# The second layer of an expert: two of its three blocks by seven half-width products

## The chip, the cores and the metric

The kernel runs on one core of a Trainium2 chip. The metric is the device time of one execution in microseconds (us). Engines are named as the profile names them: PE is TensorE, DVE VectorE, ACT ScalarE, POOL GpSimd, SP SyncE (which issues the DMAs).

## What is computed

A gated linear attention makes the rows x, a mixture of experts follows. All is fp32 at the interface.

```python
# q, k, v, f_logit: (4, 8, 768, 48)
f = sigmoid(f_logit)
for t in range(768):
    state = f[:, :, t, :, None] * state + einsum('bhd,bhe->bhde', k[:, :, t], v[:, :, t])
    y[:, :, t] = einsum('bhd,bhde->bhe', q[:, :, t], state)
x = y.transpose(0, 2, 1, 3).reshape(3072, 384)

P = exp(x @ w_gate - max)               # 3072 x 8, then 8 rounds of row and column normalisation
for e in range(8):
    h = maximum(x @ w1[e], 0)           # w1[e]: 384 x 1024
    out += P[:, e:e + 1] * (h @ w2[e])  # w2[e]: 1024 x 384
```

## The kernel before

**Products.** Each fp32 product is made of three fp16 ones: both factors are split into a high and a low part (names that end in h and l), and high by high, low by high and high by low are accumulated in PSUM. `mm` issues every matmul; all of them carry its line, L285 (L287 after).

**Stages.** Up to about 491 us the attention, the gate and experts 0 and 1 are computed. Then comes the main loop over `ORDER`: 48 periods, one for each of experts 2 to 7, half m of their 1024 hidden units, and batch b of 768 rows. A period n does layer one of its (e, m, b), and the layer two of period n−1.

**Layer one** treats the 768 rows as three blocks t of 256 tokens and the weights as a grid of blocks too, and gets all from 15 products (`SLOTS`), each 128 columns of weights (twice, c = 0 and 1) by 256 tokens: 15 x 2 x 3 = 90 matmuls of 256 columns. They go into six PSUM banks A to F, tiles kb_n_A to kb_n_F. `EVENTS` says after which slot which step on the banks follows; slots 15 to 21 are slots 0 to 6 of the next period (`pending`). The steps, in `event`: copy of a bank to a tile cp (ACT, L1354), add of such a copy to a bank (DVE, L1356), init of a bank from another and a copy (DVE, L1359), move of bank B into C (ACT, L1362), sum (DVE, L1365). A bank ends as one hidden block, half f of the columns and token block t: then hh makes kh, the high fp16 part after the maximum with 0 (ACT, L1384), and hl makes kl, the low part (DVE, L1387).

**Layer two** (`layer2`) has two ways for a block of 256 tokens. `plain(t, v)` makes 128 rows by 12 matmuls of 384 columns into a PSUM tile kyps. `paired(t)` makes both its 128-row halves at once by seven products instead of eight, each 192 columns wide, in 42 matmuls, into two PSUM tiles kxps and kyps (px and py), each with two halves (x0, x1, y0, y1). Its left factors are kah and kal (one half of the block: ga, ACT L1376; gb, DVE L1378) and four sums and differences kf of the hidden halves (hs makes kr on ACT, L1370; gs makes the four kf on DVE, L1374), split into kgh (gh, ACT L1380) and kgl (gl, POOL L1382; DVE in the last period). Its right factors are w2 and four sums of its blocks, k2s, split into k2sh and k2sl. While the products run, ACT copies three of them into part (L1240), POOL adds parts and makes one half of both (L1249, L1250), DVE makes the other half (L1252); when the products are done, DVE adds both to x1 (L1255) and to py (L1259). Block 1 is paired; blocks 0 and 2 are plain.

**Eviction.** Results go to acc, scaled by the gate: either by one DVE instruction (direct, L1211), or by ACT into yt (L1214) and POOL's add (L1215). Two of the six halves of a period are direct.

**Order.** `pin` chains instructions on DVE, ACT and POOL in the order of the code, `mm` does so on PE. `layer2` is a generator which `drain` advances after each slot by a fixed number of units, so that layer-two matmuls stand between layer-one products; it is started at slot `LAG` = 2. `postpone` puts a step off by so many slots. The table `plan` (through `at_slots`) gives to slots what else is done: weight preparation for later periods (`prepare_w1`; `prepare_w2`; `prepare_pairs`, which loads w2 a second time as k2rs and makes the sums k2s), conversion of the last batch's rows (`converts[3]`, xah3 and xal3), adding back the first two experts' results from DRAM (`readds`), and checks of the inputs' ranges (`guard`, `first_maxima`, `verdict`) that set a flag.

Of the kernel before, what the change touches and what calls it, by code (L numbers as in the profile page):

```python
# [73 lines left out]
END = 22  # L74
ORDER = [(e, m, b) for e in range(2, NE) for m in range(2) for b in range(B)]
PLAIN, PAIRED = (0, 2), 1
# [180 lines left out]
def fast(ctx, tc, qkf, vbd, wg, w1, w2, out, flag):  # L257
# [565 lines left out]
    def verdict():  # L823
# [14 lines left out]
        for n, (col, op) in enumerate(((5, ALU.min), (4, ALU.max), (2, ALU.max), (6, ALU.min), (0, ALU.min))):  # L838
            rows.append(partition_reduce(nc, cst, psm, "m", identf, g[:, col:col + 1], op, f"gd{n}", mm, pin))
            yield  # L840
            yield
# [170 lines left out]
    def prepare_w1(e, j):  # L1012
# [10 lines left out]
        for part in (WSUMS[:5], WSUMS[5:]):  # L1023
# [19 lines left out]
    def prepare_w2(e, j, maxima_last=False):  # L1043
# [6 lines left out]
        if not maxima_last:  # L1050
            maxima_()
        wh, wl = (lp.tile([128, 2, DM], F16, name=f"k2{n}_{e}_{j}", tag=f"k2{n}", bufs=4) for n in "hl")
        pin(nc.scalar.activation(out=wh, in_=raw, func=AF.Copy, scale=W2S))
        yield
        for g in range(2):
            pin(nc.vector.scalar_tensor_tensor(out=wl[:, g], in0=raw[:, g], scalar=W2S, in1=wh[:, g], op0=ALU.mult, op1=ALU.subtract))
            if g:
                k2[e, j] = wh, wl
            yield
        if maxima_last:  # L1060
            maxima_()
            yield

    def prepare_pairs(e, j):
        raw = raw_weights(e, 2, j, "s")
        yield
        sums = raw_tile(f"k2s_{e}_{j}").rearrange("p (r d) -> p r d", d=DH)
        (b11, b12), (b21, b22) = ((raw[:, f, 0:DH], raw[:, f, DH:DM]) for f in range(2))
        for n, x, op, y in ((0, b12, ALU.subtract, b22), (1, b12, ALU.subtract, b11)):
            pin(nc.gpsimd.tensor_tensor(out=sums[:, n, :], in0=x, in1=y, op=op))  # L1070
        yield
        for n, x, op, y in ((2, b11, ALU.subtract, sums[:, 0, :]), (3, b21, ALU.subtract, sums[:, 2, :])):
            pin(nc.gpsimd.tensor_tensor(out=sums[:, n, :], in0=x, in1=y, op=op))
        yield
        wh, wl = (lp.tile([128, 4, DH], F16, name=f"k2s{n}_{e}_{j}", tag=f"k2s{n}", bufs=2) for n in "hl")
        pin(nc.scalar.activation(out=wh, in_=sums, func=AF.Copy, scale=W2S))
        yield
        pin(nc.vector.scalar_tensor_tensor(out=wl, in0=sums, scalar=W2S, in1=wh, op0=ALU.mult, op1=ALU.subtract))
        k2s[e, j] = wh, wl
        yield  # L1080
# [32 lines left out]
    while True:  # L1113
# [18 lines left out]
        if step == 46:  # L1132
            work.append(chained(prepare_w1(ORDER[0][0], j) for j in range(2)))
# [35 lines left out]
    def layer2(n, h):  # L1169
# [17 lines left out]
        def plain(t, v):  # L1187
            ps = room(f"kyps_{n}_{t}_{v}")
            i = 0
            for f in range(2):  # L1190
                for c in range(2):
                    wh, wl = k2[e, 2 * m + c]
                    hh, hl = h[f, t]
                    for a, w in ((hh, wh), (hl, wh), (hh, wl)):
                        mm(out=ps, lhsT=a[:, c, 128 * v:128 * v + 128], rhs=w[:, f, :], start=(i == 0), stop=(i == 11))
                        i += 1
                        if i < 12:
                            yield 1
# [19 lines left out]
        def product(out, left, right, start=False, stop=False):  # L1218
            for c in range(2):
                if left is None:  # L1220
                    a = [x[:, c, :] for x in h['a']]
                elif left[0] is None:
                    a = [x[:, left[1], c, :] for x in h['g']]
                else:
                    a = [x[:, c, 128 * left[1]:128 * left[1] + 128] for x in h[1, PAIRED]]
# [8 lines left out]
        def paired(t=PAIRED):  # L1234
            px, py = (room(f"k{q}ps_{n}").rearrange("p (s d) -> p s d", s=2) for q in "xy")
            x0, x1, y0, y1 = (ps[:, i, :] for ps in (px, py) for i in range(2))
            part, both = (lp.tile([128, k, DH], F32, name=f"{x}_{n}", tag=x, bufs=1) for x, k in (("part", 3), ("both", 2)))
# [4 lines left out]
            yield from product(x0, None, (0, 0), start=True)  # L1242
            yield from product(x1, (None, 1), (None, 1))
            copy(0, x0)
            yield from product(y0, (None, 0), (None, 0), start=True)
            copy(1, x1)
            yield from product(y1, (None, 2), (None, 2))
# [3 lines left out]
            yield from product(x0, (1, 0), (1, 0))  # L1251
            pin(nc.vector.tensor_tensor(out=both[:, 0, :], in0=y1, in1=part[:, 0, :], op=ALU.add))  # L1252
            yield from product(x1, (None, 3), (1, 1), stop=True)
            yield from product(y0, (1, 1), (None, 3), stop=True)
# [3 lines left out]
            late = n < len(ORDER) - 1  # L1258
            postpone(late, lambda: pin(nc.vector.tensor_tensor(out=py, in0=py, in1=both, op=ALU.add)))  # L1259
# [4 lines left out]
        ends = len(halves) - (n == len(ORDER) - 1)  # L1264
        for half in halves[:ends]:
            yield from plain(*half)
        yield from paired()
        for half in halves[ends:]:
            yield from plain(*half)
# [35 lines left out]

    for n, (e, m, b) in enumerate(ORDER):
        q, c = n // 4, n % 2
        if q + 1 < PERIODS // 4 and not c:
            e2, m2, _ = ORDER[n + 4]
            gen = prepare_w1(e2, 2 * m2 + n % 4 // 2)  # L1310
            at_slots(n, (0, 5, 5, 6, 9, 11, 13) if n else (0, 5, 5), gen)
            at_slots(n + 1, (2, 5, 7, 11, 12, 13, 14) if not n else (11, 13, 14) if not n % 4 else (4, 6, 8), gen)
        if n == 0:
            at_slots(0, (1, 2, 4, 5, 12), prepare_w2(e, 2 * m, True))
            late_w2 = prepare_w2(e, 2 * m + 1, True)
            at_slots(0, (4, 6, 8, 11), late_w2)
# [181 lines left out]
```

## Time and profile before

| | |
|---|---|
| median of 3 runs | 1522.49 us (1522.18 to 1523.27) |
| the profiled execution | 1523.2 us |
| its span in the trace, mean granted clock | 1521.5 us, 0.996 |
| main loop's first matmul of bank F, period 2 | 546.27 us |
| the same, period 43 | 1413.34 us |
| last matmul of the main part | 1512.04 us |

Starts in the trace count from the span's start. A row of a timeline has start, duration, engine, line, operation, tile written, tiles read, shape, count, and in brackets the idle time before it with what ended it. A row of a group has count, busy time, mean duration in ns, idle time before and what ended it. Tile names have their numbers left out there, so kf stands for kf of all periods.

### The profile page before, as it was taken

Reading aid. Unit: us, or ns where it says so; the run is one execution under the profiler, and the core shown is the slowest. Engines: PE = TensorE matmul, PEld = TensorE weight load, DVE = VectorE, ACT = ScalarE, POOL = GpSimd, SP = SyncE. Lnnn points to the kernel's source line nnn. Section 1 sums busy time; section 2 is a strip of 40 time slices with the busy share of each in tenths; the row PEclk is TensorE's granted clock in tenths of the full one; section 3 lists DMA queues with packets and bytes.
Section 4 is the critical chain, followed back from the end, with each engine's and each line's share of the span. In section 5 each row is a group of like instructions: output and inputs, shape, how many; then the busy total and the mean of one; then the engine's idle time right before and its main releaser. Section 6 shows DMA issues by size and latency. Waiting matters only on the chain.

```text
span 1521.5 us, 35282 instructions
## 1 busy us (share of the span) xinstructions
PE 1495.7 (98%) x14321; PEld 1159.2 (76%) x14321; DVE 1146.4 (75%) x2014; ACT 903.8 (59%) x1815; POOL 764.0 (50%) x964
## 2 busy tenths in 40 slices
PE   7999999999999999999999999999999999999997
PEld 5788877666666787788877888788887888878885
DVE  8878888985775877877777777768677776767664
ACT  6655555653343766666666666666566656566553
POOL 1244444546429245566665656455454545454433
PEclk9999999999999999999999999999999999999999
DMA  9455554541001122222222121101020101010012
GB/s 277 113 136 134 136 129 112 141 115 34 27 22 63 53 75 64 66 58 83 64 79 69 58 74 33 53 21 54 22 63 12 42 22 42 23 32 22 11 59 71
DMA packets 86239, 105.15 MB, mean 69 GB/s; under 512 B 50256, under 2 KB 66768, under 8 KB 86064
## 3 DMA queue, kind: packets, MB, share of 16 engines
q1 hardware_dynamic: 86064, 102.78, 24.2%
q8 instruction: 114, 1.87, 0.5%
q14 instruction: 61, 0.50, 0.1%
HBM read 78.97 MB, written 14.16 MB: 61 GB/s over the span
## 4 chain that ended last, share of the span: by engine, by line
PE 91%; DVE 5%; ACT 1%; issue 1%; POOL 0%; DMA 0%; POOLq 0%; DVEq 0%; ACTq 0%
PE kyps L285 29%; PE yps L285 13%; PE hps L285 10%; PE kb_A L285 8%; PE kb_B L285 8%; PE kxps L285 6%; PE kb_D L285 6%; PE kb_C L285 4%; PE kb_E L285 2%; PE kb_F L285 2%; PE kvps L285 1%; PE aps L285 1%; DVE w2l L357 0%; DVE hl L438 0%; DVE w1l L357 0%
## 5 line engine op out<-in xcount | busy, mean ns | idle before, releaser
L1215 POOL TENSOR_TENSOR acc<-acc,yt 128x384 f32<-128x384 f32 x175 | 176.7, 1010 | 303.2 <-ACT yt L1214 186.3
L285 PEld LDWEIGHTS <-k1h 128*128 128x128 f16 x2880 | 281.7, 98 | 52.7
L285 PE MATMUL kyps<-k2h,kh 128*128 128x384 f16 x768 | 250.4, 326 | 0.1
L285 PE MATMUL kyps<-k2h,kl 128*128 128x384 f16 x768 | 250.4, 326 | 0.0
L285 PE MATMUL kyps<-k2l,kh 128*128 128x384 f16 x768 | 250.4, 326 | 0.0
L285 PEld LDWEIGHTS <-kh 128*128 128x128 f16 x1920 | 186.4, 98 | 67.2
L1214 ACT ACTIVATE yt<-kyps,pes 128x384 f32<-128x384 f32 x175 | 101.6, 581 | 122.5 <-PE kyps L285 81.0
L285 PEld LDWEIGHTS <-k1l 128*128 128x128 f16 x1440 | 140.8, 98 | 43.4 <-issue 7.9
L285 PE MATMUL yps<-w2h,hl 128*128 128x384 f16 x384 | 125.4, 327 | 2.8 <-DVE hl L438 2.6
L285 PE MATMUL yps<-w2l,hh 128*128 128x384 f16 x384 | 125.5, 327 | 1.9 <-DVE w2l L357 1.9
L285 PE MATMUL yps<-w2h,hh 128*128 128x384 f16 x384 | 125.5, 327 | 0.2 <-ACT hh L435 0.2
L285 PEld LDWEIGHTS <-w1h 128*128 128x128 f16 x1344 | 97.1, 98 | 34.1 <-issue 3.1
L1382 POOL TENSOR_TENSOR kgl<-kf,kgh 128x512 f16<-128x512 f32 x94 | 111.8, 1189 | 19.0 <-DVE kl L1387 11.1
L285 PEld LDWEIGHTS <-kl 128*128 128x128 f16 x960 | 93.9, 98 | 32.3 <-issue 0.3
L285 PEld LDWEIGHTS <-hh 128*128 128x128 f16 x768 | 74.6, 98 | 47.7 <-issue 2.5
L1354 ACT ACTIVATE cp<-kb_A 128x512 f32<-128x512 f32 x144 | 86.1, 598 | 25.9 <-DVE kb_A L1356 24.6
L285 PE MATMUL hps<-xl,w1h 128*128 128x128 f16 (+1 forms) x672 | 84.1, 257 | 1.2 <-DVE xl L647 0.6
L285 PE MATMUL hps<-xh,w1l 128*128 128x128 f16 (+1 forms) x672 | 84.9, 258 | 0.0
L285 PE MATMUL hps<-xh,w1h 128*128 128x128 f16 (+1 forms) x672 | 83.6, 257 | 0.4 <-DVE hl L389 0.3
L285 PE MATMUL kb_A<-xbh,k1h 128*128 128x256 f16 x288 | 78.5, 272 | 0.5 <-ACT cp L1354 0.4
L285 PE MATMUL kb_A<-xbl,k1h 128*128 128x256 f16 x288 | 78.5, 273 | 0.0
L285 PE MATMUL kb_A<-xbh,k1l 128*128 128x256 f16 x288 | 78.5, 273 | 0.0
(291 smaller groups left out, 4516.9 us busy)
## 6 DMA issues: line engine op xcount, KB each, us to landing
q<-in_qkf_dram SPq DMA_DIRECT2D x23, 672.0 KB, 5.2
vr<-in_vbd_dram SPq DMA_DIRECT2D x24, 384.0 KB, 3.5
k1r<-in_w_dram SPq DMA_DIRECT2D x24, 384.0 KB, 3.1
ys<-yr SPq DMA_DIRECT2D x48, 192.0 KB, 2.8
k2r<-in_w_dram SPq DMA_DIRECT2D x24, 384.0 KB, 3.1
yb<-ys SPq DMA_DIRECT2D x48, 192.0 KB, 2.4
k2rs<-in_w_dram SPq DMA_DIRECT2D x24, 384.0 KB, 3.0
out_dram<-acc SPq DMA_DIRECT2D x24, 192.0 KB, 1.9
```

Of the source, the lines that this page charges most:

```text
L285: ins = (nc.tensor.transpose if transpose else nc.tensor.matmul)(**kw)
L1214: pin(nc.scalar.activation(out=yt, in_=ps, func=AF.Copy, scale=p))
L1215: pin(nc.gpsimd.tensor_tensor(out=y, in0=y, in1=yt, op=ALU.add))
L1354: pin(nc.scalar.activation(out=fresh(ev[2]), in_=bk, func=AF.Copy))
L1382: pin((nc.vector if tag == str(PERIODS - 1) else nc.gpsimd).tensor_tensor(out=hs['g'][1][:, ev[1]:ev[2]], in0=hs['f'][:, ev[1]:ev[2]], in1 ...
```

## The change

Blocks 0 and 1 are paired, block 2 alone is plain. Per period 24 matmuls of 384 columns go and 42 of 192 come. The order inside a layer two is now paired(0), two plain halves, paired(1); in the first period the plain halves come first, in the last the second plain half comes last. Block 0's step hs to gl are done from banks A and B, those of block 1 as before from E and C, and block 0's first half has no kh and kl any more. The py add follows the eviction of px in the same step, and the eviction of py the step after; they were one and two steps late.

The raw w2 is loaded once: `prepare_w2` makes k2 and k2s from one load, `prepare_pairs` goes. The slots of the weight preparation, the conversion of the last batch, the readds (two per period from period 3 on), the maxima and the checks are new. The five matmuls of `verdict` are issued between layer-two matmuls of the last three periods. At the end of the loop the remaining steps follow the order `ENDING`.

```diff
+EVENTS = {..., 8: (('move', 'C', 'B'), ('hs', 'A', 0)),
+          9: (('ga', 'A', 0),), 10: (('copy', 'C', 7), ('gs', 'A', 0, 0), ('gb', 'A', 0)), 11: (('add', 'D', '-', 7),),
+          12: (('init', 'F', '+', 1, 'D'), ('hh', 'B', 1, 0)), 13: (('gs', 'B', 0, 1), ('gs', 'B', 0, 2), ('gs', 'B', 0, 3)),
+          14: (('gh', 0, 0, 2), ('gl', 0, 0, 2), ('sum', 'D', '-', 4, 3), ('hl', 'B', 1, 0)), 15: (('add', 'C', '+', 3), ('hh', 'D', 1, 2), ('gh', 0, 2, 4), ('gl', 0, 2, 4)),
+          16: (('hh', 'C', 1, 1), ('hh', 'F', 0, 2), ('hl', 'D', 1, 2), ('ga', 'E', 1)), 17: (('hs', 'E', 1), ('hl', 'F', 0, 2)),
+          18: (('gs', 'E', 1, 0), ('gb', 'E', 1)), 19: (('gs', 'C', 1, 1), ('gs', 'C', 1, 2), ('gs', 'C', 1, 3)),
+          20: (('gh', 1, 0, 2), ('gl', 1, 0, 2), ('hl', 'C', 1, 1)), 21: (('gh', 1, 2, 4), ('gl', 1, 2, 4))}
+ENDING = (('add', 'gh', 'gl'), ('ga', 'hs', 'hh'), ('gs',), ('gb', 'hl'), ('gh', 'gl', 'late'))
-PLAIN, PAIRED = (0, 2), 1
+PLAIN, PAIRED = (2,), (0, 1)
...
-            late = n < len(ORDER) - 1
-            postpone(late, lambda: pin(nc.vector.tensor_tensor(out=py, in0=py, in1=both, op=ALU.add)))
-            postpone(2 * late, lambda: evict(t, 1, py, False))
+            pin(nc.vector.tensor_tensor(out=py, in0=py, in1=both, op=ALU.add))
+            postpone(n < len(ORDER) - 1, lambda: evict(t, 1, py, False))
             yield PAUSE
-        halves = [(t, v) for t in PLAIN for v in range(2)]
...
+        parts = [lambda: paired(0), lambda: plain(2, 0), lambda: plain(2, 1), lambda: paired(1)]
+        if n == len(ORDER) - 1:
+            parts[2:] = parts[:1:-1]
+        if not n:
+            parts = parts[1:3] + parts[::3]
+        for part in parts:
+            yield from part()
...
-            drain((24 * len(PLAIN) + 42 * PAIR_COST + PAUSE) / PRODUCTS)
+            drain((24 * len(PLAIN) + (42 * PAIR_COST + PAUSE) * len(PAIRED)) / PRODUCTS)
```

What this does to the order, at three places. First DVE where period 8 passes into period 9, and period 7's layer two ends. Before, from the half of both to kl of bank F:

```order
L1252 TENSOR_TENSOR both_7_10919<-kyps_7_10917,part_7_10918 128x192
L1356 TENSOR_TENSOR kb_8_C_10842<-kb_8_C_10842,cp8_3_10980 128x512
L1255 TENSOR_TENSOR kxps_7_10916<-kxps_7_10916,both_7_10919 128x192
L1211 SCALAR_TENSOR_TENSOR acc3_9480<-kxps_7_10916,pes_114,acc3_9480 128x384
L1374 SCALAR_TENSOR_TENSOR kf_8_10861<-kb_8_C_10842,kr_8_10864 128x256
L1374 SCALAR_TENSOR_TENSOR kf_8_10861<-kb_8_C_10842,kf_8_10861 128x256 x2
L1259 TENSOR_TENSOR kyps_7_10917<-kyps_7_10917,both_7_10919 128x384
L1387 SCALAR_TENSOR_TENSOR kl_8_1_2_10678<-kb_8_D_10749,kh_8_1_2_10677 128x512
L1387 SCALAR_TENSOR_TENSOR kl_8_1_1_10676<-kb_8_C_10842,kh_8_1_1_10675 128x512
L1356 TENSOR_TENSOR kb_9_A_11009<-kb_9_A_11009,cp9_13_11049 128x512
L1387 SCALAR_TENSOR_TENSOR kl_8_0_2_10672<-kb_8_F_10930,kh_8_0_2_10671 128x512
```

After, over the same steps (the number behind the period is the block):

```order
L1364 TENSOR_TENSOR cp8_3_11260<-kb_8_D_11029,cp8_4_10963 128x512
L1392 SCALAR_TENSOR_TENSOR kl_8_1_0_10928<-kb_8_B_10956,kh_8_1_0_10927 128x512
L1257 TENSOR_TENSOR both_7_1_11200<-kyps_7_1_11198,part_7_1_11199 128x192
L1355 TENSOR_TENSOR kb_8_C_11118<-kb_8_C_11118,cp8_3_11260 128x512
L1392 SCALAR_TENSOR_TENSOR kl_8_1_2_10932<-kb_8_D_11029,kh_8_1_2_10931 128x512
L1260 TENSOR_TENSOR kxps_7_1_11197<-kxps_7_1_11197,both_7_1_11200 128x192
L1216 SCALAR_TENSOR_TENSOR acc3_9594<-kxps_7_1_11197,pes_114,acc3_9594 128x384
L1263 TENSOR_TENSOR kyps_7_1_11198<-kyps_7_1_11198,both_7_1_11200 128x384
L1392 SCALAR_TENSOR_TENSOR kl_8_0_2_10926<-kb_8_F_11209,kh_8_0_2_10925 128x512
L1355 TENSOR_TENSOR kb_9_A_11285<-kb_9_A_11285,cp9_13_11335 128x512
L1375 SCALAR_TENSOR_TENSOR kf_8_1_11337<-kb_8_E_11063,kr_8_1_11340 128x256
```

The py add (kyps) now follows the eviction of kxps at once, ahead of kl of F and the add to kb_9_A; kl of D moved ahead of the x1 add, and the kf of C went behind.

Second, DVE in period 1, from the add to bank A to the add to bank B. Before:

```order
L1356 TENSOR_TENSOR kb_1_A_8530<-kb_1_A_8530,cp1_13_8562 128x512
L992 TENSOR_TENSOR xal3_8554<-xs0_3_8132,xah3_8553 128x768
L1387 SCALAR_TENSOR_TENSOR kl_0_0_2_8345<-kb_0_F_8492,kh_0_0_2_8344 128x512
L1078 SCALAR_TENSOR_TENSOR k2sl_2_0_8568<-k2s_2_0_8496,k2sh_2_0_8567 128x768
L1359 TENSOR_TENSOR kb_1_E_8624<-kb_1_D_8594,cp1_6_8601 128x512
L992 TENSOR_TENSOR xal3_8554<-xs0_3_8132,xah3_8553 128x768
L1207 TENSOR_SCALAR acc0_8570<-kyps_0_0_1_8614,pes_114 128x384
L1356 TENSOR_TENSOR kb_1_B_8540<-kb_1_B_8540,cp1_0_8645 128x512
```

After:

```order
L1355 TENSOR_TENSOR kb_1_A_8519<-kb_1_A_8519,cp1_13_8554 128x512
L1375 SCALAR_TENSOR_TENSOR kf_0_1_8556<-kb_0_E_8406,kr_0_1_8559 128x256
L1381 SCALAR_TENSOR_TENSOR kal_0_1_8543<-kb_0_E_8406,kah_0_1_8542 128x256
L993 TENSOR_TENSOR xal3_8546<-xs0_3_8132,xah3_8545 128x768
L1375 SCALAR_TENSOR_TENSOR kf_0_1_8556<-kb_0_C_8434,kr_0_1_8559 128x256
L1375 SCALAR_TENSOR_TENSOR kf_0_1_8556<-kb_0_C_8434,kf_0_1_8556 128x256 x2
L1081 SCALAR_TENSOR_TENSOR k2sl_2_0_8567<-k2s_2_0_8441,k2sh_2_0_8566 128x768
L1358 TENSOR_TENSOR kb_1_E_8629<-kb_1_D_8598,cp1_6_8605 128x512
L1392 SCALAR_TENSOR_TENSOR kl_0_1_1_8347<-kb_0_C_8434,kh_0_1_1_8346 128x512
L1081 SCALAR_TENSOR_TENSOR k2sl_2_1_8589<-k2s_2_1_8475,k2sh_2_1_8588 128x768
L993 TENSOR_TENSOR xal3_8546<-xs0_3_8132,xah3_8545 128x768
L1355 TENSOR_TENSOR kb_1_B_8530<-kb_1_B_8530,cp1_0_8648 128x512
```

Four kf and one kal of block 1 and a second k2sl stand between the two adds, and the eviction acc0 no longer does.

Third, ACT at the end of the loop, from kh of the last bank on. Before:

```order
L1384 ACTIVATE kh_47_0_2_22435<-kb_47_F_22658 128x512
L1214 ACTIVATE yt_46_1_1_22733<-kyps_46_22645,pes_114 128x384
L1214 ACTIVATE yt_47_0_0_22749<-kyps_47_0_0_22731,pes_114 128x384
L1380 ACTIVATE kgh_47_22600<-kf_47_22599 128x512 x2
L1214 ACTIVATE yt_47_2_0_22788<-kyps_47_2_0_22771,pes_114 128x384
L1240 ACTIVATE part_47_22794<-kxps_47_22792 128x192 x2
L1240 ACTIVATE part_47_22794<-kyps_47_22793 128x192
L1214 ACTIVATE yt_47_1_1_22848<-kyps_47_22793,pes_114 128x384
```

After:

```order
L1389 ACTIVATE kh_47_0_2_24250<-kb_47_F_24520 128x512
L1378 ACTIVATE kah_47_1_24599<-kb_47_E_24386 128x256
L1370 ACTIVATE kr_47_1_24605<-kb_47_E_24386 128x512
L1219 ACTIVATE yt_46_1_1_24607<-kyps_46_1_24509,pes_114 128x384
L1245 ACTIVATE part_47_0_24613<-kxps_47_0_24611 128x192 x2
L1245 ACTIVATE part_47_0_24613<-kyps_47_0_24612 128x192
L1219 ACTIVATE yt_47_0_1_24675<-kyps_47_0_24612,pes_114 128x384
L1384 ACTIVATE kgh_47_1_24603<-kf_47_1_24602 128x512 x2
L1219 ACTIVATE yt_47_2_0_24705<-kyps_47_2_0_24679,pes_114 128x384
L1245 ACTIVATE part_47_1_24711<-kxps_47_1_24709 128x192 x2
L1245 ACTIVATE part_47_1_24711<-kyps_47_1_24710 128x192
L1219 ACTIVATE yt_47_1_1_24765<-kyps_47_1_24710,pes_114 128x384
```

kah and kr of block 1 follow the last kh, and the last block's kgh stand behind the eviction yt of paired(0)'s py.

More of the change, by code (lines that the diff above doesn't have):

```diff
@@ L1438, in fast @@
     lowers += layers
-    for first_ in (True, False):
-        for evs in pending:
-            for ev in evs:
-                if (ev[1][0] in ('add', 'hh', 'hl', 'ga', 'gb')) == first_:
-                    event(*ev)
-            due()
-            drain(24 * len(PLAIN) / len(pending) / 2)
+    rest = [ev for evs in pending for ev in evs]
+    for kinds in ENDING:
+        for ev in rest:
+            if ev[1][0] in kinds and (ev[1][0] not in ('gh', 'gl') or (ev[1][1] == 1) == ('late' in kinds)):
+                event(*ev)
+        due()
+        drain(48 / len(ENDING))
     for lower in lowers:
```

166 lines of the change are left out of this document (81 added, 85 removed), and 7 rows, old and new, of the table EVENTS.

## The prediction

> **What bounds the kernel now.** I read the page's busy line and its chain of waits first, then the TensorE rows of single periods, then busy time by stretches, then the groups by shape.
>
> ```profile
> span 1521.5 us, 35282 instructions
> PE 1495.7 (98%) x14321; PEld 1159.2 (76%) x14321; DVE 1146.4 (75%) x2014; ACT 903.8 (59%) x1815; POOL 764.0 (50%) x964
> PE 91%; DVE 5%; ACT 1%; issue 1%; POOL 0%; DMA 0%; POOLq 0%; DVEq 0%; ACTq 0%
> ```
>
> TensorE is busy nearly throughout and makes up 91% of the chain that ends last. A busy TensorE need not be one at its pace, so the pace comes from starts. Below are the first matmul of bank F in periods 2 and 43, then places where matmuls of one width follow each other: 12 of 256 columns from 1014.98, 36 of 384 from 1500.93, 42 of 192 from 1506.78.
>
> ```profile
> 546.27 0.27 PE L285 MATMUL kb_F<-xah,k1h 128*128 128x256 f16 x1
> 1413.34 0.27 PE L285 MATMUL kb_F<-xah,k1h 128*128 128x256 f16 x1
> ...
> 1014.98 0.27 PE L285 MATMUL kb_B<-xbh,k1h 128*128 128x256 f16 x1
> 1016.29 0.33 PE L285 MATMUL kyps<-k2h,kh 128*128 128x384 f16 x1
> ...
> 1500.93 0.33 PE L285 MATMUL kyps<-k2h,kh 128*128 128x384 f16 x1
> 1506.78 0.25 PE L285 MATMUL kxps<-k2h,kah 128*128 128x192 f16 x1
> 1510.25 0.33 PE L285 MATMUL kyps<-k2h,kh 128*128 128x384 f16 x1
> ```
>
> From start to start that is 1.31/12 = 0.109 us, 5.85/36 = 0.1625 us and 3.47/42 = 0.0826 us. A period of before has 90, 48 and 42 of them: 9.81 + 7.80 + 3.47 = 21.08 us. Measured are (1413.34 − 546.27)/41 = 21.15 us, so in the steady loop TensorE loses only some 0.07 us per period. The loop is bound by TensorE's issue pace; what the other engines have free is the second question.
>
> ```profile
> core 0: us, PE busy (x) PEld busy (x) DVE busy (x) ACT busy (x) POOL busy (x), PEclk, DMA share, GB/s
> 609.78:694.65 84.87, 84.80 (x723) 67.84 (x721) 64.60 (x111) 56.40 (x114) 53.19 (x70) 1.00 0.23 67
> 1012.11:1096.57 84.46, 84.46 (x722) 67.86 (x721) 62.03 (x109) 51.77 (x104) 43.23 (x61) 1.00 0.13 39
> 503.08:525.18 22.10, 20.31 (x164) 15.37 (x162) 20.24 (x33) 16.83 (x32) 8.80 (x10) 1.00 0.24 72
> ```
>
> The first two are four periods each. VectorE is busy 16.2 and 15.5 us per period, ScalarE 14.1 and 12.9, GpSimd 13.3 and 10.8; the granted clock is 1.00. The third is the first full period: TensorE idles 1.8 of 22.1 us there, and VectorE is nearly full.
>
> **The change part by part.** *Matmuls.* Every period loses 24 matmuls of 384 columns and gains 42 of 192: 24 × 0.1625 − 42 × 0.0826 = 3.90 − 3.47 = 0.43 us. Over 48 periods that is −20.9 us, if TensorE stays the bound; the period becomes 20.65 us. The Trainium skill, TensorE: Matmul & The Clock Gate, section Back-to-back issue gap, says that the spacing in a stream of loads and matmuls grows slowly with width, 81 ns at 128 columns and 131 ns at 512; a straight line between gives, as an estimate, 89 ns at 192 and 114 ns at 384, by which 42 for 24 would cost 1.0 us more per period and the time would rise by 48 us. The trace disagrees, since its 384 take 0.1625 us against 0.0826 us, almost in proportion.
>
> *The elementwise work of the second paired block.* Prices by shape:
>
> ```profile
> L1374 DVE SCALAR_TENSOR_TENSOR kf<-kb_C,kf 128x256 f32<-128x256 f32 x96 | 40.3, 420 | 1.6
> L1378 DVE SCALAR_TENSOR_TENSOR kal<-kb_E,kah 128x256 f16<-128x256 f32 x48 | 19.9, 415 | 0.0
> L1252 DVE TENSOR_TENSOR both<-kyps,part 128x192 f32<-128x192 f32 x48 | 17.2, 358 | 47.8 <-ACT part L1240 47.7
> L1255 DVE TENSOR_TENSOR kxps<-kxps,both 128x192 f32<-128x192 f32 x48 | 17.6, 366 | 12.8 <-PE kxps L285 12.6
> L1259 DVE TENSOR_TENSOR kyps<-kyps,both 128x384 f32<-128x384 f32 x48 | 26.7, 556 | 0.0
> L1387 DVE SCALAR_TENSOR_TENSOR kl<-kb_A,kh 128x512 f16<-128x512 f32 x48 | 33.2, 691 | 56.6 <-ACT kh L1384 56.6
> L1370 ACT ACTIVATE kr<-kb_E 128x512 f32<-128x512 f32 x48 | 28.5, 594 | 0.2 <-ACT kh L1384 0.2
> L1376 ACT ACTIVATE kah<-kb_E 128x256 f16<-128x256 f32 x48 | 18.5, 386 | 0.0
> L1380 ACT ACTIVATE kgh<-kf 128x512 f16<-128x512 f32 x96 | 60.4, 629 | 0.1
> L1240 ACT ACTIVATE part<-kxps 128x192 f32<-128x192 f32 x96 | 28.6, 327 | 19.3 <-PE kxps L285 18.9
> L1382 POOL TENSOR_TENSOR kgl<-kf,kgh 128x512 f16<-128x512 f32 x94 | 111.8, 1189 | 19.0 <-DVE kl L1387 11.1 <-ACT kgh L1380 7.9
> L1249 POOL TENSOR_TENSOR part<-part 128x192 f32<-128x192 f32 x48 | 28.3, 591 | 96.7 <-ACT part L1240 96.0 <-POOL acc L1215 0.7
> ```
>
> VectorE gains four kf, one kal, both, the x1 add and the py add and loses one kl: 1.68 + 0.42 + 0.36 + 0.37 + 0.56 − 0.69 = 2.70 us. ScalarE gains kr, kah, two kgh and three part and loses one kh (as kr): 0.39 + 1.26 + 0.98 = 2.63 us. GpSimd gains two kgl and two sums: 2.38 + 1.18 = 3.56 us. So early in the loop VectorE comes to 18.9 us of 20.65 (91%), ScalarE to 16.7 (81%), GpSimd to 16.9 (82%); in mid loop to 18.2, 15.6 and 14.4. Nobody overflows on average, so I cost this at nothing; its cover is the remaining 1.8 us of VectorE. How accumulators are evicted stays two by VectorE and four by ScalarE with GpSimd.
>
> *The hand-over.* `paired(1)` now ends a period's layer two and `paired(0)` of the next follows, so the same pair of PSUM banks is written again soon; between them stand only 18 matmuls (six of y0, twelve of layer one), 6 × 0.0826 + 12 × 0.109 = 1.80 us. What must be done in that time shows at the end of before, where the same steps stand together:
>
> ```profile
> 1500.29 0.69 DVE L1356 TENSOR_TENSOR kb_C<-kb_C,cp 128x512 f32<-128x512 f32 x1
> 1500.36 0.25 PE L285 MATMUL kxps<-k2l,kgh 128*128 128x192 f16 x1
> 1500.88 0.36 DVE L1255 TENSOR_TENSOR kxps<-kxps,both 128x192 f32<-128x192 f32 x1
> 1501.27 0.62 DVE L1211 SCALAR_TENSOR_TENSOR acc<-kxps,pes,acc 128x384 f32<-128x384 f32 x1
> ```
>
> From the start of the last x1 matmul to the end of the eviction pass 1.53 us, and TensorE needs 1.88 us to come back. The slack is 0.35 us: cost nothing at the likeliest, up to 0.4 us per period if VectorE runs late (its queue ahead of the add holds both, kb_C's add and a kl). The py add moves one step forward and now waits for GpSimd's sum; the sums wait for the third part, two products (1 us) and the x1 and y0 products (1 us) ahead of it, against 1.18 us of work: about 0.8 us of room. Behind it on VectorE stand kl of F and the next add to bank A, then TensorE.
>
> *The old small stall.* The 0.07 us per period comes mostly from bank D's last products waiting for VectorE's init of F; in the new order F's init is not behind kf, kal. It goes or stays: 0 to −2.6 us, I take −1.0.
>
> *Raw weights once.* This removes 24 loads of 384 KB and makes the sums in the same pass; GpSimd, ScalarE and VectorE do the same conversions as before.
>
> ```profile
> k2rs<-in_w_dram SPq DMA_DIRECT2D x24, 384.0 KB, 3.0
> L1078 DVE SCALAR_TENSOR_TENSOR k2sl<-k2s,k2sh 128x768 f16<-128x768 f32 x24 | 30.2, 1260 | 0.0
> ```
>
> With the DMA share at 0.13 to 0.24 the transfers hid behind TensorE; zero. Readds, maxima, guard steps and conversions are the same instructions in other slots, and the verdict's five matmuls move a few periods; zero, their cover again the spare VectorE time.
>
> *The start.* In period 1 VectorE gains four kf, a kal, a second k2sl and loses an acc eviction between the adds to banks A and B: 1.68 + 0.42 + 1.26 − 0.6 = 2.8 us by records against 1.9 us of idle time in the window above. +1 us, from 0 to +3.
>
> *The end.* After the last layer one product TensorE's remaining work is short and VectorE's list long. If bank C's add starts at 1500.29 as before, on the old clock, VectorE goes through kgl, x1 add, acc, py add, four kf, both, three kl, kal, x1 add, acc, py add. Starts of these in before are 0.3 to 0.8 us apart:
>
> ```profile
> 1503.00 0.56 DVE L1259 TENSOR_TENSOR kyps<-kyps,both 128x384 f32<-128x384 f32 x1
> 1503.47 0.68 DVE L1387 SCALAR_TENSOR_TENSOR kl<-kb_F,kh 128x512 f16<-128x512 f32 x1
> 1504.07 0.41 DVE L1374 SCALAR_TENSOR_TENSOR kf<-kb_C,kr 128x256 f32<-128x256 f32 x1
> 1504.40 0.88 DVE L1374 SCALAR_TENSOR_TENSOR kf<-kb_C,kf 128x256 f32<-128x256 f32 x2
> 1505.71 1.65 DVE L1382 TENSOR_TENSOR kgl<-kf,kgh 128x512 f16<-128x512 f32 x2
> 1511.48 0.58 ACT L1214 ACTIVATE yt<-kyps,pes 128x384 f32<-128x384 f32 x1 [2.19 <-DVE kyps L1259]
> ```
>
> That is kb_C 0.6, kgl 0.8, x1 0.4, acc 0.5, py 0.5, kf 1.3, both 0.3, kl 1.8, kal 0.3, x1 0.4, acc 0.5, py 0.5 = 7.9 us, to 1508.2. Then ScalarE, in order, does yt (0.58) and the first kgh of the last block (0.7), and VectorE the first kgl (0.8): 1510.3. TensorE arrives at that product after paired(0), a plain half and one product: 1500.93 + 3.47 + 1.95 + 0.50 = 1506.85. A wait of 3.5 us, not there before; +1 if VectorE's queue is shorter at that time, +4.5 with hand-offs. I take +3.5.
>
> *Sum:* −20.9 − 1.0 + 1.0 + 3.5 = −17.4 us. The profiled execution took 1523.2 us for its span of 1521.5, 0.7 above the median 1522.49; the difference is applied to the median: 1505.1 us.
>
> **The rivals.** A is the forecast; its own range is −22.5 (start 0, end +1, stall gone) to −13 us (start +3, end +4.5, stall unchanged), 1500 to 1510.
>
> B: the hand-over. VectorE reaches the x1 add 0.35 us or more late in most periods, because at 88 to 91% it is rarely idle, and bank px comes free after TensorE wants it. For it: the slack is smaller than one 0.69 us kl. Against: VectorE idles 12.8 us over the 48 x1 adds, waiting for TensorE. A stall of 0.25 us (0.1 to 0.4) over 47 periods returns 12 us: 1517; from 0.43 us per period on nothing is gained.
>
> C, the other side: the py add waits for GpSimd. Its sums stand behind a kgl of 1.19 us and accumulations of 1 us; when these come late, VectorE stands at the py add with kl and the add to bank A behind it, and TensorE's next period waits. For it: GpSimd reaches 82% and was idle 96.0 us waiting for the parts, so it is in step with them only by its free time. Against: that free time. It becomes slower than before when TensorE waits over 0.43 us per period, that is when GpSimd is late by the 0.8 us of room and the rest that VectorE can give; one kgl late, 1.19 us, less 0.35 us of slack makes 0.8 us per period, +38 us less 17: 1543.
>
> D, the weight loads: each matmul has one.
>
> ```profile
> L285 PEld LDWEIGHTS <-kgh 128*128 128x128 f16 x768 | 71.4, 98 | 1.6
> ```
>
> Were they to follow each other without overlap, 216 × 98 ns = 21.2 us would bound a period, as long as now: with start and end 1527. Against it: 768 × 98 ns = 75.3 us exceed the 71.4 us in which they were busy, and the half-width matmuls go at 0.0826 us already. The Trainium skill, Perfetto Trace Analysis, section Identifying the Most-Contended Engine, would judge TensorE by this row and not by its busy time; the trace shows 76% there, and 192-column stretches beyond it.
>
> **How the numbers follow.** A 0.77, B 0.14, C 0.05, D 0.04. The time is A's, 1505.1 us. The range goes from A's low end, 1500, into the lower part of B, 1514, and leaves out half of B, C, D and little of A, some 0.18. About 0.2%, 3 us, is what a measurement of this kernel can tell from no change. Faster takes A and three quarters of B, 0.87; same the stall of 0.4 us in B, 0.04; slower C and D, 0.09.
>
> **What would show it.** From F to F 20.65 us in mid loop, with VectorE at 88% of it: the matmul term. A gap ahead of the first kxps of each period: B. Idle VectorE ahead of the py add put down to GpSimd's both, and a late bank A: C. 192-column starts over 0.09 us apart: D. Period 1 over 23 us: the start is dearer than taken. In the last 15 us, a TensorE gap ahead of kxps<-k2sh,kgl that VectorE's kgl ends: the end term. The prediction falls if VectorE's real order leaves TensorE waiting for add, init or move of a bank in every period, which none of my slack counts covers.

## The result, and the profile after

The changed kernel took 1511.59 us (median of 4 runs, 1510.53 to 1511.74) against 1522.88 us of the kernel before in the same session: a ratio of 0.9925, 95% interval 0.9907 to 0.9942. That is 11.3 us faster, where 17.4 us were forecast. Direction and range held; a third of the gain is missing, and the question is where it went.

The page's first lines, busy times and the chain:

```profile
span 1510.0 us, 37891 instructions
PE 1477.1 (98%) x15185; PEld 1213.1 (80%) x15185; DVE 1282.7 (85%) x2352; ACT 1002.8 (66%) x2103; POOL 968.4 (64%) x1154
PE 88%; DVE 7%; ACT 2%; issue 1%; POOL 1%; DMA 1%; DVEq 0%; POOLq 0%; ACTq 0%
```

TensorE is still busy for 98% and leads the chain, but VectorE's part of the chain rose from 5 to 7%. Now the same two kinds of stretches as before the change: the TensorE rows with bank F's first matmul of periods 0, 1, 2, 5, 20, 21, 45 and 47, and four periods early in the loop.

```profile
503.41 0.27 PE L287 MATMUL kb_F<-xah,k1h 128*128 128x256 f16 x1
525.53 0.27 PE L287 MATMUL kb_F<-xah,k1h 128*128 128x256 f16 x1
550.37 0.27 PE L287 MATMUL kb_F<-xah,k1h 128*128 128x256 f16 x1
614.87 0.27 PE L287 MATMUL kb_F<-xah,k1h 128*128 128x256 f16 x1
924.70 0.27 PE L287 MATMUL kb_F<-xah,k1h 128*128 128x256 f16 x1
946.63 0.27 PE L287 MATMUL kb_F<-xah,k1h 128*128 128x256 f16 x1
1442.35 0.27 PE L287 MATMUL kb_F<-xah,k1h 128*128 128x256 f16 x1
1484.84 0.27 PE L287 MATMUL kb_F<-xah,k1h 128*128 128x256 f16 x1
```

```profile
594.26:676.90 82.64, 82.64 (x793) 72.16 (x792) 74.99 (x142) 63.81 (x137) 67.26 (x83) 1.00 0.20 55
```

Period n is counted here from F of n to F of n+1; F is the last bank of a period to start, so the stretch holds mostly layer one of period n+1. From period 5 to 20 it is (924.70 − 614.87)/15 = 20.66 us, from 21 to 45 (1442.35 − 946.63)/24 = 20.66 us: TensorE's own sum, and no wait. The columns of the second fence are those of the stretches shown before the change; TensorE's busy time equals the stretch, VectorE is at 75.0/82.64 = 91%. But periods 0 to 4 took 614.87 − 503.41 = 111.46 us instead of 5 × 20.65 = 103.25: **8.2 us are lost in the first five periods**. Before, the same five took 106.71 us against 105.4 of work, 1.3 us lost. Period 20 loses 1.3 us more, and from period 45 to 47 the distance is 42.49 us, 1.2 above two periods, at the verdict's matmuls (gd_t). After the last F comes the end, whose last matmul starts at:

```profile
1501.74 0.33 PE L287 MATMUL kyps<-k2l,kh 128*128 128x384 f16 x1
```

16.90 us after F, against 1512.04 − 1498.71 = 13.33 before. What TensorE waited for from 503.5 to 594.1 us, periods 0 to 3 (engine, line, what it waited for: total, times, longest):

```profile
PE kyps L287 <- DVE both L1257: 2.4, 1, 2.4
PE kyps L287 <- DVE acc L1212: 1.2, 1, 1.2
PE kxps L287 <- ACT part L1245: 0.8, 2, 0.4
PE kb_D L287 <- DVE kb_F L1358: 0.4, 1, 0.4
PE kyps L287 <- DVE kl L1392: 0.4, 1, 0.4
```

Two single waits make up almost half, and both are ended by VectorE. Smaller ones and a slower clock (below) are the rest. VectorE's timeline up to the end of the longest, which lies where period 1 passes into period 2, then GpSimd's beside it:

```profile
525.10 0.87 DVE L1375 SCALAR_TENSOR_TENSOR kf<-kb_B,kf 128x256 f32<-128x256 f32 x2
525.89 0.81 DVE L1039 SCALAR_TENSOR_TENSOR k1l<-k1s,k1h 128x640 f16<-128x640 f32 x1
526.62 1.65 DVE L993 TENSOR_TENSOR xbl<-xs,xbh 128x512 f16<-128x512 f32 x1
528.19 0.68 DVE L1364 TENSOR_TENSOR cp<-kb_D,cp 128x512 f32<-128x512 f32 x1
528.79 0.68 DVE L1392 SCALAR_TENSOR_TENSOR kl<-kb_B,kh 128x512 f16<-128x512 f32 x1
529.39 0.81 DVE L1039 SCALAR_TENSOR_TENSOR k1l<-k1s,k1h 128x640 f16<-128x640 f32 x1
530.12 0.35 DVE L1257 TENSOR_TENSOR both<-kyps,part 128x192 f32<-128x192 f32 x1
```

```profile
526.20 1.52 POOL L1387 TENSOR_TENSOR kgl<-kf,kgh 128x512 f16<-128x512 f32 x1 [5.55 <-ACT kgh L1384]
527.68 1.03 POOL L1254 TENSOR_TENSOR part<-part 128x192 f32<-128x192 f32 x1
```

VectorE is busy without a gap, but with k1l, xbl and k1l, conversions that nobody needs for some periods. The step TensorE waits for, both, is 0.35 us long and stands last. And xbl takes 1.65 us here, while GpSimd works on kgl and part.

### The profile page after: what moved, and what is told of

The parts are those of the page before. It is cut to its first block, busy times and chain, and to the rows that moved or that the text cites. A ratio compares the mean times of both kernels' runs of the same rounds, so it can differ in the third digit from the quotient of the medians.

```text
span 1510.0 us, 37891 instructions
## 1 busy us (share of the span) xinstructions
PE 1477.1 (98%) x15185; PEld 1213.1 (80%) x15185; DVE 1282.7 (85%) x2352; ACT 1002.8 (66%) x2103; POOL 968.4 (64%) x1154
## 4 chain that ended last, share of the span: by engine, by line
PE 88%; DVE 7%; ACT 2%; issue 1%; POOL 1%; DMA 1%; DVEq 0%; POOLq 0%; ACTq 0%
PE kyps L287 21%; PE yps L287 13%; PE kxps L287 12%; PE hps L287 10%; PE kb_A L287 8%; PE kb_B L287 8%; PE kb_D L287 6%; PE kb_C L287 4%; PE kb_E L287 2%; PE kb_F L287 2%; PE kvps L287 1%; PE aps L287 1%; DMA w1r<-in_w_dram 1%; DVE kf L1375 1%; POOL k1s L1026 0%
## 5 line engine op out<-in xcount | busy, mean ns | idle before, releaser
L1387 POOL TENSOR_TENSOR kgl<-kf,kgh 128x512 f16<-128x512 f32 x188 | 217.1, 1165 | 40.9 <-ACT kgh L1384 40.2
L287 PEld LDWEIGHTS <-kgh 128*128 128x128 f16 x1536 | 144.3, 98 | 5.3 <-ACT kgh L1384 1.1
L287 PE MATMUL kyps<-k2h,kh 128*128 128x384 f16 x384 | 125.2, 326 | 1.5 <-DVE acc L1212 1.2
L287 PE MATMUL kyps<-k2h,kl 128*128 128x384 f16 x384 | 125.2, 326 | 0.4 <-DVE kl L1392 0.4
L287 PE MATMUL kyps<-k2l,kh 128*128 128x384 f16 x384 | 125.2, 326 | 0.0
L1384 ACT ACTIVATE kgh<-kf 128x512 f16<-128x512 f32 x192 | 120.7, 629 | 3.6 <-DVE kf L1375 3.5
L1254 POOL TENSOR_TENSOR part<-part 128x192 f32<-128x192 f32 x96 | 57.3, 596 | 88.7 <-DVE kf L1375 61.1
L1353 ACT ACTIVATE cp<-kb_A 128x512 f32<-128x512 f32 x144 | 87.4, 607 | 21.9 <-PE kb_A L287 21.6
L287 PE MATMUL kyps<-k2sl,kgh 128*128 128x192 f16 x384 | 94.5, 246 | 0.0
L287 PE MATMUL kyps<-k2sh,kgl 128*128 128x192 f16 x384 | 94.5, 246 | 0.0
L287 PE MATMUL kyps<-k2sh,kgh 128*128 128x192 f16 x384 | 94.5, 246 | 0.0
```

What stands on the lines that cost most here:

```text
L287: ins = (nc.tensor.transpose if transpose else nc.tensor.matmul)(**kw)
L1254: pin(nc.gpsimd.tensor_tensor(out=part[:, 1, :], in0=part[:, 1, :], in1=part[:, 2, :], op=ALU.add))
L1353: pin(nc.scalar.activation(out=fresh(ev[2]), in_=bk, func=AF.Copy))
L1384: pin(nc.scalar.activation(out=hs['g', t][0][:, lo:hi], in_=hs['f', t][:, lo:hi], func=AF.Copy))
L1387: pin((nc.vector if tag == str(PERIODS - 1) else nc.gpsimd).tensor_tensor(out=hs['g', t][1][:, lo:hi], in0=hs['f', t][:, lo:hi], in1=hs['g ...
```

## The experiments

**Is it VectorE's load, or the new slots?** Theory L: the first periods have too much VectorE work for a second paired block. Theory P: the new slots of preparation and conversion lose the time, whatever layer two does. The first two kernels went back to one paired block, once in periods 0 to 3, once everywhere, under the new slots:

```diff
+OLD_EVENTS = {...}
+ONE = frozenset(range(4))
...
+        if n in ONE:
+            parts = [lambda: plain(0, 0), lambda: plain(0, 1), lambda: plain(2, 0), lambda: plain(2, 1), lambda: paired(1)]
...
-            for ev in EVENTS.get(s, ()):
+            for ev in (OLD_EVENTS if n in ONE else EVENTS).get(s, ()):
```

`OLD_EVENTS` are the steps of before; in the second kernel `ONE` is all 48 periods.

> The changed kernel, but in periods 0 to 3 only block 1 is paired (block 0 plain, with the steps hh and hl of before); both blocks are paired from period 4 on. Theory L (load): the 8.2 us that TensorE loses in periods 0 to 4 come from VectorE, which has the conversions of the last batch, two sets of weights and the maxima to do there and cannot take 2.1 us more per period. It expects these losses to fall to about 1.5 us, against 4 x 0.435 = 1.7 us more of matmuls: 1511.6 - 6.7 + 1.7 = 1506.6 us. Theory P (places): the losses come from the new slots of the weight preparation and conversion, whatever layer two does. It expects them to stay at 8 us: 1513.3 us.

> The new slots of preparation, conversion and checks, the single load of w2 and the new end order, but with one paired block in all periods, as before. Theory L: periods 0 to 4 lose 1 to 3 us in all, as before the change, and the rest is as before: 1522 to 1525 us. Theory P: periods 0 to 4 lose about 8 us: 1529 to 1531 us. The small stall of bank D in every other period (2.6 us in all before, none after) should come back if it hangs on where kf and kal stand in VectorE's order, and stay away if it hung on the slots of the preparation.

Measured: 1516.6 and 1612.4 us, neither theory. The waits of ScalarE in the second kernel, between 700 and 800 us, show why:

```profile
ACT kah L1391 <- PE kxps L295: 13.1, 4, 3.3
```

The change takes one buffer of kah per block instead of two, and in the order of before kah is written while the last paired block still reads the old one: up to 3.3 us of waiting in each period. In the changed kernel ga of block 1 stands six slots later, after that reading. So the later place of ga lets the change do with one buffer; these two variants lacked it. With two buffers:

> As one_first4 (one paired block in periods 0 to 3), but with the two buffers for kah and kal that the one-block order had: the run before made ScalarE wait for a buffer of kah, in all four periods, which was no part of the question. Theory L (VectorE overloaded in periods 0 to 4): the losses there fall from 8.2 us, and 1.2 us more of a slower clock, to about 2 us, against 1.7 us more of matmuls: 1506 us. Theory P (the new slots of preparation and conversion): they stay: 1513 us.

> As one_all (all the other parts of the change, one paired block throughout), with the two buffers for kah and kal. Theory L: 1521 to 1525 us, 1 to 3 us lost in periods 0 to 4. Theory P: 1529 us or more, 8 us lost there. Steady periods of 21.09 us; the small stall of bank D in every other period is back if it hangs on the order of VectorE's steps on the banks.

Measured: 1509.28 us (ratio 0.9914, 0.9897 to 0.9930) and 1524.44 us (1.0015, 1.0005 to 1.0024). The first stands between the theories; 10.3 us of it lie behind the last matmul, against 8.3 in the changed kernel, for a reason that stays open. The second lies in L's range, and so do the 2.7 us that it loses from F to F in periods 0 to 4 (108.14 against 105.4). Counted matmul by matmul from the first product to about 589 us, TensorE loses 4.9 us in the kernel before, 7.5 in either of these two, and 12.2 in the changed kernel. So of the 7.3 us more, 2.6 come with the new slots alone, and 4.7 with the second block on top of them; 1.3 of the 4.7 are the slower clock, by tail3 below, which ran without it. The bank D stall came back in part only: 0.04 us per period in the second kernel.

**The py add.**

> The changed kernel with the py add one step and the eviction of py two steps later again, as before the change. Theory L expects no difference above 0.7 us (1511.6 us), steady periods 20.66 us. Rival C, that the py add waiting for GpSimd's sum holds up VectorE, has no stalls in the steady loop to explain but could make the start: it expects 2 us or more less, 1509.5 us or below.

The edit gives the py add and its eviction back their one and two steps of delay. Measured 1511.01 us (1510.3 to 1512.1), steady periods 20.66 us, period 1 unchanged at 24.8 us. Rival C of the prediction has no part in it.

**Less work at the start.** If the load counts, any VectorE work taken away there should do:

> The changed kernel; the maxima of the four w2 tiles of expert 2 are not taken in periods 0 to 3 but later, from four loads more, in the slots of the maxima of experts 0 and 1. This takes 4 x 0.94 = 3.8 us from VectorE at the start and moves nothing else. Theory L expects the losses of periods 0 to 4 to fall by 2 to 3.5 us, and the slower clock of period 1 to go with its long wait: 1507 to 1509.5 us. Rival S: the waits there are ended by VectorE only in name, and ScalarE and GpSimd set them: no change above 0.7 us.

Measured 1510.70 us (1509.72 to 1511.40): 0.9 us, less than half of the 2 us that L expected at the least, and a little over the 0.7 of S. 1.0 us was gained ahead of the first F; the long wait went from 2.36 to 2.08 us only, although a maximum of 0.94 us ahead of it had gone. Ahead of the kf steps VectorE now idled 0.48 us for ScalarE, and the three conversions still stood between kf and both. That is not what a sum of work predicts, and it split L in two.

**The same work in another place.**

```diff
-            at_all(n, (...) if n else (14, 17, 18, 19, 20, 24, 25, 26, 27, 28, 29, 37), gen)   # prepare_w1
+            at_all(n, (...) if n else (14, 17, 18, 19, 20, 24, 25, 26, 27, 32, 34, 37), gen)
-            ... (0, 2, 8, 12, 13, 16, 16, 17, 20), prepare_w2(...)
+            ... (0, 2, 8, 12, 13, 16, 16, 17, 24), prepare_w2(...)
-    at_all(1, (1, 3, 6, 8, 11, 13, 14, 18, 21, 23, 26, 28, 29), converts[3])
+    at_all(1, (1, 3, 6, 8, 11, 18, 21, 23, 26, 28, 29), converts[3])
```

> The changed kernel with four pieces of VectorE's movable work in other slots and nothing taken away: the last half of the last batch's low part (xbl) and two conversions k1l, which stand ahead of both in period 1, go some five slots later, and one k2sl of period 4 goes from slot 5 to slot 9. After the last runs theory L is split. L1 (the sum of the work): VectorE is full there, so what is moved makes TensorE wait a little later; the gain is at most 1 us: 1510.6 us or more. L2 (what stands ahead of the one step that TensorE waits for): the wait of 2.4 us ahead of kyps<-k2sh,kh and that of 1.2 us at kyps<-k2h,kh shrink to under 0.6 us, and with the first the slower clock goes: 1511.4 - 2 - 1 - 1.2 = 1507.2 us.

Measured 1507.30 us (1507.05 to 1507.48; ratio 0.9900, 0.9883 to 0.9916), where L2 said 1507.2. VectorE's timeline at the same place, and TensorE's longest waits from 503.3 to 594.1 us:

```profile
525.85 0.68 DVE L1364 TENSOR_TENSOR cp<-kb_D,cp 128x512 f32<-128x512 f32 x1
526.45 0.68 DVE L1392 SCALAR_TENSOR_TENSOR kl<-kb_B,kh 128x512 f16<-128x512 f32 x1
527.05 0.34 DVE L1257 TENSOR_TENSOR both<-kyps,part 128x192 f32<-128x192 f32 x1
...
532.49 0.68 DVE L993 TENSOR_TENSOR xbl<-xs,xbh 128x512 f16<-128x512 f32 x1
```

```profile
PE kxps L287 <- ACT part L1245: 1.0, 2, 0.6
PE kyps L287 <- DVE both L1257: 0.5, 1, 0.5
```

both comes 3.1 us earlier, with the same instructions, and xbl takes 0.68 us in its new place. The two long waits are gone and nothing comparable took their place: period 1 is 21.6 us instead of 24.8, period 3 21.1 instead of 22.5. From F to F periods 0 to 4 took 107.05 us instead of 111.46. Of these 4.4 us some 1.3 are the slower clock, which went with the wait. So most of the added loss was the order: what stood ahead of one short step. Part of the gain is that xbl got out of GpSimd's way, which this run doesn't separate, and 2.5 us more than before the change stay lost in these periods (3.8 against 1.3), which no experiment took away.

**How much room has the hand-over?** The prediction counted 0.35 us between the eviction of px and its next use.

```diff
             pin(nc.vector.tensor_tensor(out=x1, in0=x1, in1=both[:, 0, :], op=ALU.add))
+            if t == 1 and 8 <= n < 44:
+                for _ in range(3):
+                    pin(nc.vector.tensor_tensor(out=both[:, 0, :], in0=y1, in1=part[:, 0, :], op=ALU.add))
```

> The changed kernel with three more VectorE instructions of 128 x 192 (both's first half made again, with the same values) between the x1 add of paired(1) and the eviction of px, in periods 8 to 43: 3 x 0.27 = 0.81 us more on the way of bank px to paired(0) of the next period. The prediction counted 0.35 us of slack there: it expects a stall of 0.81 - 0.35 = 0.46 us per period, 36 x 0.46 = 17 us: 1528 us, TensorE waiting at the first kxps product. Rival: VectorE has enough free time ahead of the x1 add that the slack is nearer 0.8 us: no stall, 1511.6 us. If VectorE as a whole is the bound with these, the waits are spread over add, init and move as well.

Measured 1541.0 us, 13 us more than expected; steady periods of 21.43 us, 0.78 above 20.66. First VectorE in the changed kernel at this place with TensorE's next use of px, then the same in this one:

```profile
906.89 0.36 DVE L1260 TENSOR_TENSOR kxps<-kxps,both 128x192 f32<-128x192 f32 x1
907.28 0.62 DVE L1216 SCALAR_TENSOR_TENSOR acc<-kxps,pes,acc 128x384 f32<-128x384 f32 x1
...
908.31 0.25 PE L287 MATMUL kxps<-k2h,kah 128*128 128x192 f16 x1
```

```profile
721.77 0.35 DVE L1260 TENSOR_TENSOR kxps<-kxps,both 128x192 f32<-128x192 f32 x1
722.23 1.14 DVE L1263 TENSOR_TENSOR both<-kyps,part 128x192 f32<-128x192 f32 x3
723.28 0.61 DVE L1216 SCALAR_TENSOR_TENSOR acc<-kxps,pes,acc 128x384 f32<-128x384 f32 x1
...
723.95 0.26 PE L287 MATMUL kxps<-k2h,kah 128*128 128x192 f16 x1 [0.60 <-DVE acc L1216]
```

In the changed kernel the eviction ends at 907.90 and TensorE comes at 908.31: 0.41 us of room. The three instructions moved the eviction not by 0.81 but from 0.39 to 1.51 us behind the x1 add, by 1.12 us: the first started 0.46 us behind the x1 add, and the three, which write one place, started 0.39 us apart, not 0.27 (the row has them as one of 2 × 0.39 + 0.36 = 1.14). 1.12 − 0.78 = 0.34 us was absorbed. The room of 0.35 us was right; the price of the added work was not. And rival B is seen to be real: a period gains 21.15 − 20.66 = 0.49 us, so some 0.85 us more on this way gives all of it back.

**The end.**

```diff
-ENDING = (('add', 'gh', 'gl'), ('ga', 'hs', 'hh'), ('gs',), ('gb', 'hl'), ('gh', 'gl', 'late'))
+ENDING = (('add', 'gh', 'gl'), ('ga', 'hs', 'hh'), ('gs',), ('gh', 'late'), ('gb', 'hl'), ('gl', 'late'))
```

> The changed kernel; at the end ScalarE makes the last block's kgh ahead of the eviction yt of paired(0)'s py; VectorE's order is as it was. The prediction's end term says that kgh standing behind yt and py add, then kgl, makes TensorE wait before the second product of the last paired block (0.9 + 0.85 us in the trace). It expects the first of these to go and the second to shrink to 0.4 to 0.8 us: 1511.6 - 1.2 = 1510.4 us. Rival: VectorE's place for kgl alone sets it, because VectorE is busy up to then: nothing gained, 1511.6 us.

TensorE's rows at the last paired block, first of the changed kernel, then ScalarE's that end the first wait:

```profile
1490.63 0.24 PE L287 MATMUL kxps<-k2h,kh 128*128 128x192 f16 x1 [1.07 <-ACT part L1245]
1495.95 0.26 PE L287 MATMUL kxps<-k2sh,kgh 128*128 128x192 f16 x1 [0.89 <-ACT kgh L1384]
1497.05 0.26 PE L287 MATMUL kxps<-k2sh,kgl 128*128 128x192 f16 x1 [0.85 <-DVE kgl L1387]
```

```profile
1494.79 0.58 ACT L1219 ACTIVATE yt<-kyps,pes 128x384 f32<-128x384 f32 x1 [3.99 <-DVE kyps L1263]
1495.27 1.14 ACT L1384 ACTIVATE kgh<-kf 128x512 f16<-128x512 f32 x2
```

In the variant the distance from the last F to the last matmul fell from 16.90 to 15.71 us, 1.19 where 1.2 was expected; the 0.89 us went, 0.27 of the 0.85 stayed, and 0.29 came up at both (L1257). Its median, 1508.98 us (1508.73 to 1510.62), is 2.6 us lower; in its profiled execution 1.3 of that is period 1, which had no slower clock there.

**Together.**

> start2 and two more moves: at the end of the loop ScalarE makes the last block's kgh ahead of yt (as tail3) and VectorE the last block's kgl ahead of the x1 add, the eviction and the py add of paired(0), and the last lumps of the input checks are cut into four smaller ones, so that period 20 does not get 1.9 us of them. Expected against start2: the end shorter by 1.7 us than in the changed kernel, period 20 by 1.2 us: 1507.2 - 2.9 = 1504.3 us under L2, 1507.7 us under L1.

Measured 1505.78 us (1505.52 to 1505.92), where L2 gave 1504.3. Period 20 fell to 20.66 us as expected, but the checks cost 0.4 us in periods 22 and 24 (20.76 and 20.96); the end fell only to 15.97. Both waits before the last products were gone, but 1.16 us by start distances (1.00 in the row) had come up at the copies (part) that stand on ScalarE behind the same yt: in order, yt waits for the py add, and that had moved back behind kgl.

> best, and at the end of the loop two evictions wait for their turn: the yt of period 46's py is issued behind the copies (part) of paired(0) of period 47, and the yt of that one's py behind the copies of the last paired(1). In best ScalarE, in order, stood at each of these yt until VectorE had done the py add, and TensorE waited for the copies behind it: 1.24 us at paired(0), 1.16 us at paired(1). Expected: the second goes, the first goes or shrinks to what VectorE's adds allow, the end 1.2 to 2.2 us shorter: 1505.8 - 1.7 = 1504.1 us. Rival: the banks or the parts were late for another reason (GpSimd's sums), no change above 0.7 us.

Measured **1504.28 us** (1504.18 to 1504.54; ratio to before 0.9879, 0.9863 to 0.9896), the end 14.81 us, 1.16 shorter. This version does the same computation as the changed kernel and is 18.3 us faster than the kernel before, against 11.3 of the change as it was made.

## Why the prediction was right or wrong

**The range held by luck.** 1511.6 us lies outside the 1500 to 1510 that were given to the forecast's own mechanism. It lies inside the stated range because that was widened to 1514 for rival B, a stall in most periods, which did not come.

**Matmuls: right.** 20.65 us were worked out for a period, 20.66 measured; 24 wide for 42 narrow ones save the 0.43 us in full. Rival D is out: 84 half-width matmuls per period go at the pace of before. Its price was also miscounted: a period has 90 + 24 + 84 = 198 loads and not 216, and 198 × 98 ns = 19.4 us would not have bound it.

**Elementwise work: right.** VectorE 18.9 us per period forecast, 75.0/4 = 18.7 measured; ScalarE 16.7 and 16.0, GpSimd 16.9 and 16.8. The cover that was named for it, VectorE's last 1.8 us, holds throughout the steady loop.

**Hand-over: right.** 0.35 us of room worked out, 0.41 read and 0.34 measured. B happened in one period only, the 20th (below); its point of decision was as near as said. C did not happen either.

**Old stall: a little more; the checks: not free.** 2.6 us in periods 5 to 43 went to zero, where −1.0 was taken; period 20 takes 1.3 back. Its input checks stand on VectorE in two lumps, the first from 926.95 to 928.00 us, ahead of kl, the x1 add and the eviction of px:

```profile
926.95 0.21 DVE L810 TENSOR_REDUCE g<-qkm 112x1 f32<-112x64 f32 x1
...
928.60 0.35 DVE L1260 TENSOR_TENSOR kxps<-kxps,both 128x192 f32<-128x192 f32 x1
929.66 0.26 PE L287 MATMUL kxps<-k2h,kah 128*128 128x192 f16 x1 [0.53 <-DVE acc L1216]
```

TensorE's matmul starts 0.80 us behind the one ahead of it instead of 0.11. That is 0.69 us lost, where 1.05 of checks less 0.35 of room make 0.70. This is rival B's stall. The second lump stands ahead of both of the next paired block and costs the rest. The prediction counted the checks at nothing, and their cover was VectorE's spare time in general; there it was gone in two places.

**The end: right in size, in part in path.** +3.5 us forecast. Measured is +3.6 us in the distance to the last matmul, after the last layer two's own saving of 0.43, so 4.0 of waiting. The forecast had it all at the last block's first kgl. Of that chain, yt, kgh and kgl showed as said, but with 0.89 + 0.85 = 1.74 us; 1.07 us was a wait for part ahead of them, which was not named. That the sum came out so close is in part luck.

**The start: wrong, and this is the missing 6 us.** The step was "+1 us, from 0 to +3", worked out as VectorE's added work between the first two F against its idle time there. Over periods 0 to 4 it measured +6.9 us. Three things failed in it. It looked at one stretch, and there it was about right: from the first F to the second took 22.12 us after 22.10, 0.45 more than the matmuls account for. The loss came in the next stretches, 4.2 us in period 1 and 1.9 in period 3, where moving conversions was taken as free; the new slots lose 2.6 us with one block already. It compared sums of work, where the loss hangs on what stands ahead of a step that TensorE needs at once: start2 regained 4.4 us without taking away any work. And it priced each instruction at its duration of before, where xbl, 0.71 us on average, takes 1.65 beside GpSimd. A slower clock came on top, 1.3 of the 6.9.

From the last matmul to the end 8.3 us passed, against 9.4 before, a gain of 1.2 us that no step foresaw. The eleven experiments had 6.6 to 10.3 us there with the same last steps in most, so this is put down to no cause.

The ledger by these distances: matmuls of 47 periods −20.2, start +6.9, old stalls, checks and the verdict −0.9, up to the first F +0.3, end +3.6, behind it −1.2: −11.5 us, the difference of the two spans.

## What to carry to other kernels

An engine at 91% costs nothing in a steady loop that was ordered with care, and costs at once where other work of its own is laid between. So where work is added, list for each step that the bounding engine waits for what stands ahead of it on its own engine, above all where a loop starts, and put work with no due time behind such steps; a sum against idle time doesn't show it. Engines kept in a fixed order pass waits on: an eviction that waits for an add holds up what stands behind it, kgh and twice the copies at the end of this kernel and its variants.

## What the runs showed of the hardware

**The clock fell after a wait of 2.4 us.** In the changed kernel's profile TensorE's granted clock at the end of the long wait, by stretches of one microsecond (the number ahead of the last two):

```profile
530.00:531.00 1.00, 0.48 (x6) 0.47 (x6) 1.00 (x4) 0.51 (x2) 0.91 (x1) 0.92 0.00 0
531.00:532.00 1.00, 1.00 (x7) 0.73 (x5) 0.96 (x4) 0.90 (x2) 0.25 (x1) 0.50 0.09 16
533.00:534.00 1.00, 1.00 (x7) 0.72 (x6) 0.65 (x2) 1.00 (x3) 0.00 (x0) 0.50 0.00 0
534.00:535.00 1.00, 1.00 (x12) 0.97 (x11) 0.97 (x3) 1.00 (x2) 0.00 (x0) 0.87 0.00 0
```

From 530.8 to 534.2 it stood at 0.50, and matmuls of 256 columns started 0.21 us apart instead of 0.109. tail3, with the same order there and the same wait, kept 1.00, and its period 1 took 23.51 us instead of 24.84: a wait can cost half of itself again, in some executions and not in others, which also fits that runs of the changed kernel lie at 1510.5 or 1511.6. The profiles of py_late, slack3 and, after 2.08 us, maxima_late have the same stretch at 0.50. The Trainium skill, TensorE: Matmul & The Clock Gate, section What's actually happening, gives half rate after at least one idle window of about 3.4 us, in windows that run freely. Here it followed a wait of 2.36 us, with TensorE busy for some half of the time around it. That the phase of such a window decides is in line with this, and not shown.

**VectorE and GpSimd slowed each other where both of VectorE's inputs lie in SBUF.** By shape, k2l and k1l in the kernel before, then after, and kf, which reads PSUM:

```profile
L1056 DVE SCALAR_TENSOR_TENSOR k2l<-k2r,k2h 128x384 f16<-128x384 f32 x48 | 34.0, 707 | 0.0
L1038 DVE SCALAR_TENSOR_TENSOR k1l<-k1r,k1h 128x384 f16<-128x384 f32 x24 | 14.2, 593 | 0.0
```

```profile
L1053 DVE SCALAR_TENSOR_TENSOR k2l<-k2r,k2h 128x384 f16<-128x384 f32 x48 | 50.2, 1048 | 0.0
L1039 DVE SCALAR_TENSOR_TENSOR k1l<-k1r,k1h 128x384 f16<-128x384 f32 x24 | 22.1, 921 | 0.0
L1375 DVE SCALAR_TENSOR_TENSOR kf<-kb_C,kf 128x256 f32<-128x256 f32 x96 | 40.2, 419 | 1.6
```

The same instructions became 48 and 55% longer as GpSimd's busy time rose from 764 to 968 us; kf stayed at 419 against 420 ns. What counts is GpSimd's work just beside: in the kernel before, the 22 k2l that overlap no GpSimd instruction take 0.55 us each, and 22 that do for over 30% of their time 0.90 on average, up to 1.36; and k2sl went the other way, from 1260 to 1004 ns. GpSimd pays too: its sum beside xbl, 1.03 us in the row above, is the only first sum of 96 above 0.62 us. The Trainium skill, SBUF — State Buffer, section Terms, has a pair of ports that these two engines lock against each other for a whole instruction. The rows agree in direction, and xbl's 1.65 us beside kgl and part against 0.68 in start2 is the plainest case; no run varied GpSimd's work alone.
